# The first batch of an attention-then-network kernel: odd heads on the upper partitions, five first transfers, and a planner that counts transfers in flight

## The chip, the cores and the metric

The kernel runs on one core of one Trainium2 chip. The metric is the device time of one execution in microseconds. Five engines take part, each with its own in-order instruction queue: TensorE (PE; its weight loads are shown apart, as PEld), VectorE (DVE), ScalarE (ACT), GpSimd (POOL) and SyncE (SP), which here issues nearly all transfers from HBM.

## The reference, cut to what matters

Windowed attention with a linear bias for 8 batches of 8 heads, 576 positions and head size 64, then a two-layer network over all 4608 rows:

```python
scores = scale * np.matmul(q, k.transpose(0, 1, 3, 2))
bias = slopes[:, None, None] * (-np.abs(rel).astype(np.float32))[None, :, :]
mask = (rel >= 0) & (rel < window)                    # window = 128
scores = np.where(mask, scores + bias[None], -1000000000.0)
attn = softmax(scores)                                # max, exp, sum + 1e-9
x = np.matmul(attn, v) ...reshape(4608, 512)
h = x @ w_in                                          # 512 x 2048
g = h * (1.0 / (1.0 + np.exp(-1.702 * h)))
out = g @ w_out                                       # 2048 x 512
```

## The kernel before, in words

**The network.** Rows of x are taken in 18 chunks of 256 (a `Job` each; the first chunk is done in two jobs, eight of the sixteen slices of the hidden size in each). One step of a job takes one slice f of 128 hidden units: `up` (twelve matmuls into `h_ps`, L881), the gating on ACT and DVE (L889, L890), the split of g into a high and a low fp32r part (`gh`, `gl`), and `down` (six matmuls into `acc`, L905). x and the weights are split into high and low parts in the same way, so that three fp32r products stand for one fp32 product.

**The weights** arrive as 64-bit words (512 KB a slice and matrix, 32 in all) and are turned into fp32 by `decode`: two steps on ACT (L511, L513), two on DVE (L515, L518), a cast for the high part, and a subtraction for the low part, which may run on POOL or on DVE (L522, by `less_ways`). Decoding of the first two starts when `DECODE_TICK` units of attention have been written down.

**Attention.** Batches 1 to 7 work on pairs of heads in fp32r. Batch 0 is done in plain fp32, head by head, so that the network can begin early: for rows 0 to 255, then 256 to 511, then 512 to 575, eight units of one head each. A unit is: scores (`s_ps` or, for odd heads of the first rows, `s_h`, L694); bias and row minimum on DVE (L712); exponent and row sum on ACT (L724); reciprocal of the sum (L733, L735); scaling (L746 on POOL or DVE, L744 on ACT); transposes on PE (`t_ps`, L767); a copy to SBUF (`turned` or `pw`, L435); times V (`x_ps` or `x_acc`, L806); a copy into x (L850). Here Q and K of batch 0 lie on partitions 0 to 63 for every head. `load_part` fetches them in pieces of two heads (128 KB) and V in pieces of 128 rows (256 KB); the first part takes ten transfers, four of Q and two of V on SP and four of K on ACT, and the second ten on SP. Casts and copies that the planner may move are recorded at L435, such subtractions at L438, halvings at L444. The tiles lie where late weights will come to lie (`home`).

**What sets the order.** `Plan` records every operation with a cost in ns, and `order` (L280) runs through a list schedule of the five engines with these costs up to 130,000 ns of its own time (`CUT`); the instructions are then written out in that order. Its constants decide: `READY` (when an engine is first free), `LAX` (how much longer an operation may take on its first engine than on another before it is moved there), `RATE` (bytes per ns of the transfers), `AHEAD` (how far transfers may be issued ahead), `WARM` (before that time, PE's costs count double), `SLACK` (how many network steps before its due time the attention of a batch should be finished), `FETCH_AHEAD` (how many slices of weights are fetched ahead of decoding). Behind the cut, `rest` hands out the remaining operations and a scheduler places them. Where the plan leaves PE idle before the first `acc` matmul, `spins` fills in bf16 matmuls of the identity matrix (`spin`, L482, tile `idle`), whose result nothing reads, one for every 107 ns, or 214 ns in the first 7 us. They are called spins below.

Of the kernel before, what the change touches and what calls it, by code (L numbers as in the profile page):

```python
# [21 lines left out]
P = 128  # L22
# [11 lines left out]
BIG = 3.0e38  # L34
FAR = 1.0e37
DEPTH = 3
FETCH_AHEAD = 6
DECODE_AHEAD = 1
F0 = 8
SLACK = 4  # L40
DECODE_TICK = 4
AHEAD = 3000
GATE = 6
READY = {"PE": 1600, "DVE": 4400, "ACT": 2100, "POOL": 2700, "SP": 700}
HOP = {"PE": 220, "ACT": 60, "DVE": 60, "POOL": 60, "SP": 60}
CUT = 130000
WARM = 7000
LAX = {"w": 0, "hi": 800, "lo": 2000, "gl": 150, "cast": 100, "xl": 600, "p": 300}
RATE = 330
SOON = 0  # L50
NEXT = 100
SPIN = 107
MIXED = ("t", "o", "h", "acc1")
ENGINES = ("PE", "ACT", "DVE", "POOL", "SP")
# [168 lines left out]
class Plan:  # L223
# [56 lines left out]
    def order(self, until):  # L280

        free = dict(READY)
        port = 0
        wire = 0
        queue = {e: [] for e in ENGINES}
        def ahead(e, op):
            return sum(o.ns for o in queue[e] if o.n < op.n and len(o.ways) == 1)
# [9 lines left out]
        while True:  # L297
            best = None
            for e in ENGINES:
                pick = None  # L300
                for op in queue[e]:
                    at = max(op.ready, free[e], wire - AHEAD if op.bytes else 0)
                    blocked = False
                    for buf in op.opens:
                        if buf.at is None:
                            times = [0 if s is None else (s.done if s.left == 0 else None) for s in buf.slots]
                            times = [t for t in times if t is not None]
                            if not times:
                                blocked = True
                                break  # L310
                            at = max(at, min(times))
                    if blocked:
                        continue
                    ends = at + op.ways[e][0]
                    if any(max(op.ready, free[o] + ahead(o, op)) + op.ways[o][0] + op.lax < ends for o in op.ways if o != e):
                        continue
                    if pick is None or (at, op.n) < pick[:2]:
                        pick = (at, op.n, op)
                if pick:
                    at = max(pick[0], port) if pick[2].ways[e][1] else pick[0]  # L320
                    if best is None or (at, pick[0]) < best[:2]:
                        best = (at, pick[0], pick[2], e)
            if best is None or best[0] >= until:
                break
            at, _, op, op.eng = best
            op.ns, op.port = op.ways[op.eng]
            if op.eng == "PE" and at < WARM:
                op.ns *= 2
            for e in op.ways:
                queue[e].remove(op)  # L330
            for buf in op.opens:
                free_at = [(0 if s is None else s.done, i) for i, s in enumerate(buf.slots) if s is None or s.left == 0]
# [64 lines left out]
def tile_kernel(ctx: ExitStack, tc: tile.TileContext, q0, k0, v0, qT, kT, v, w_in, w_out, out):  # L397
# [16 lines left out]

    def spins(a, b):
        cold = max(min(b, WARM) - a, 0)
        return int(cold // (2 * SPIN) + (b - max(a, min(b, WARM))) // SPIN)

    def act_cast(n):
        return 104 + 0.8 * n  # L420
# [116 lines left out]
            yield hh, c, o, at, m  # L537
            at += m

    homes = [f"w{i}_{f}" for f in range(NF - 1, NF - 12, -1) for i in (1, 2)]  # L540
    parts, values = {}, {}

    def home(shape, name):
        return buf(const, shape, F32, homes.pop(), name=name)

    def load_part(lo, n, on=("SP", "SP")):
        if n == T:
            Q = [home([P, 4, T], f"q{lo}_{i}") for i in range(2)]
            K = [home([P, 4, T], f"k{lo}_{i}") for i in range(2)]
            parts[lo // T] = Q, K  # L550
            V = home([P, 2, DM], f"v{lo}")
            for j in range(2):
                values[lo // P + j] = (V, j), lambda h, j=j: V.t[:, j, h * D:(h + 1) * D]
            for i in range(4):
                for e, (src, to) in zip(on, ((q0, Q), (k0, K))):
                    st = to[i // 2]
                    hs = slice(i % 2 * 2, i % 2 * 2 + 2)
                    piece(e, st, src[:, 2 * i:2 * i + 2, lo:lo + n], lambda t, hs=hs: t[:D, hs], 131072, i % 2)
                if i == 1:
                    for j in range(2):  # L560
                        piece("SP", V, v0[lo + j * P:lo + j * P + P, :], lambda t, j=j: t[:, j], 262144, j)
        else:
            QK = home([P, 2, H, n], f"qk{lo}")
            parts[lo // T] = [QK], [QK]
            V = home([P, DM], f"v{lo}")
            values[lo // P] = (V, 0), lambda h: V.t[:n, h * D:(h + 1) * D]
            piece("SP", QK, q0[:, :, lo:lo + n], lambda t: t[:D, 0], 131072, 0)
            piece("SP", QK, k0[:, :, lo:lo + n], lambda t: t[:D, 1], 131072, 1)
            piece("SP", V, v0[lo:lo + n, :], lambda t: t[:n], 131072, 0)

    def piece(e, dst, src, view, bytes, name):
        on = nc.sync if e == "SP" else nc.scalar
        add(e, lambda: on.dma_start(view(dst.t), src), 550 if e == "SP" else 110, w=[(dst, name)], bytes=bytes,
            chain="first" + e)

    def columns(kind, h, lo, n):
        i, at = divmod(lo, T)
        to = parts[i][kind]
        if len(to) == 2:
            st = to[h // 4]  # L580
            return (st, h // 2 % 2), lambda: st.t[:D, h % 4, at:at + n]
        return (to[0], kind), lambda: to[0].t[:D, kind, h, at:at + n]

    def load(u):
        if u.whole:
# [497 lines left out]
def lay_out(q, k, v, moe_w_in, moe_w_out):  # L1083
# [7 lines left out]
    def words(w):  # L1091
        return np.ascontiguousarray(w).view(np.int64)

    def rows(a):

        return np.ascontiguousarray(np.asarray(a)[0].transpose(2, 0, 1))
# [4 lines left out]
    return {  # L1101
        "q0": rows(q),
        "k0": rows(k),
        "v0": np.ascontiguousarray(v[0].transpose(1, 0, 2)).reshape(S, DM),
        "qT": transposed(q[1:]),
        "kT": transposed(k[1:]),
# [16 lines left out]
```

## Time and profile before

| | |
|---|---|
| median of 3 runs (lowest, highest) | 1073.58 us (1073.49, 1073.8) |
| the profiled execution | 1070.47 us, its span 1068.5 us |
| mean granted TensorE clock | 0.995 |
| PE busy, share of the span | 1054.0 us, 99% |
| DVE, ACT, POOL busy | 737.1, 611.7, 575.5 us |
| first `h_ps` matmul | 39.19 us |

The span runs from the first to the last instruction. A timeline row gives start, duration, engine, line, operation and tiles, and in brackets the idle time before it with what ended it. The granted clock is a share of full speed. A line number is that of the kernel before; "x4" counts instructions. An fp32 matmul shows as two records.

### The profile page before, as it was taken

What the parts mean: (1) busy time and instruction counts of PE and PEld (TensorE: products, weight loads), DVE (VectorE), ACT (ScalarE), POOL (GpSimd) and SP (SyncE); (2) the same over time, 40 slices, a digit from 0 to 9 for tenths busy, and PEclk for the clock granted to TensorE, in tenths of its full rate; (3) what the DMA queues carried; (4) which work ended last, traced back from release to release, by engine and by line L of the source; (5) the groups of instructions that cost most, each with busy time, mean ns of one, the idle gap of its engine ahead of it and who ended that gap; (6) DMA issues with size and microseconds to landing.
All of it is one profiled execution on the core that took longest, in us unless ns stands there. A gap on an engine that the chain in (4) does not pass through costs nothing.

```text
span 1068.5 us, 21819 instructions
## 1 busy us (share of the span) xinstructions
PE 1054.0 (99%) x7044; PEld 943.7 (88%) x7044; DVE 737.1 (69%) x2339; ACT 611.7 (57%) x1817; POOL 575.5 (54%) x871
## 2 busy tenths in 40 slices
PE   8999999999999999999999999999999999999998
PEld 5768899998999899999999998999899989998987
DVE  5999999889886777634778668785878677313121
ACT  5988976666666565524565556655566555322222
POOL 1324576677676666533566557665666565323232
PEclk8999999999999999999999999999999999999999
DMA  9922423333332232201222212221322120000000
GB/s 236 361 81 94 128 73 83 100 81 97 83 90 64 71 88 56 83 9 39 54 86 61 81 54 87 67 84 45 93 67 73 52 66 30 21 1 21 1 21 20
DMA packets 90272, 80.18 MB, mean 75 GB/s; under 512 B 42992, under 2 KB 80880, under 8 KB 90160
## 3 DMA queue, kind: packets, MB, share of 16 engines
q1 hardware_dynamic: 84400, 68.84, 22.4%
q10 hardware_dynamic: 5760, 9.96, 2.6%
q8 instruction: 55, 0.90, 0.3%
q14 instruction: 57, 0.47, 0.1%
HBM read 69.34 MB, written 9.44 MB: 74 GB/s over the span
## 4 chain that ended last, share of the span: by engine, by line
PE 88%; DVE 6%; ACT 3%; issue 2%; DMA 1%; POOL 0%; ACTq 0%; DVEq 0%; SPq 0%
PE h_ps L881 35%; PE acc L905 35%; PE t_ps L767 5%; PE x_ps L812 5%; PE s_ps L697 5%; PE x_ps L806 1%; PE s_ps L694 1%; DVE pb L712 1%; DVE K L435 1%; DVE pb L746 1%; DVE xh L435 1%; DMA k<-k 0%; DMA rw<-w_in 0%; ACT rw L513 0%; DVE xf L852 0%
## 5 line engine op out<-in xcount | busy, mean ns | idle before, releaser
L881 PE MATMUL h_ps<-xh,w 128*128 128x256 f32 x2304 | 371.2, 284 | 2.1 <-DVE rec L733 0.8
L881 PEld LDWEIGHTS h_ps<-xh,w 128*128 128x128 f32 x2304 | 327.8, 188 | 29.1 <-DVE g L890 1.4
L438 POOL TENSOR_TENSOR gl<-g,gh 128x256 fp32r<-128x256 f32 x275 | 204.6, 744 | 269.6 <-ACT gh L435 207.9
L905 PE MATMUL acc<-w,gh 128*128 128x512 f32 x1152 | 325.7, 398 | 0.8 <-ACT gh L435 0.8
L890 DVE SCALAR_TENSOR_TENSOR g<-g,h_ps 128x256 f32<-128x256 f32 x288 | 119.6, 415 | 188.7 <-ACT g L889 187.0
L889 ACT ACTIVATE g<-h_ps 128x256 f32<-128x256 f32 x288 | 110.0, 382 | 204.8 <-PE h_ps L881 176.4
L905 PEld LDWEIGHTS acc<-w,gh 128*128 128x128 f32 x1152 | 195.7, 188 | 27.1 <-ACT gh L435 1.3
L881 PE MATMUL h_ps<-xl,w 128*128 128x256 f32 x1152 | 196.5, 282 | 0.0
L435 ACT CAST gh<-g 128x256 fp32r<-128x256 f32 x283 | 114.5, 405 | 132.1 <-DVE g L890 121.3
L905 PE MATMUL acc<-w,gl 128*128 128x512 f32 x576 | 188.2, 401 | 0.0
L881 PEld LDWEIGHTS h_ps<-xl,w 128*128 128x128 f32 x1152 | 164.4, 188 | 6.6 <-DVE xl L438 0.2
L438 POOL TENSOR_TENSOR K<-rk,K 128x384 fp32r<-128x384 f32 (+1 forms) x140 | 128.0, 915 | 77.2 <-PE s_ps L697 14.5
L724 ACT ACTIVATE pb<-pb,mins 128x256 f32<-128x256 f32 (+3 forms) x276 | 134.2, 487 | 61.3 <-DVE mins L712 59.2
L746 DVE TENSOR_SCALAR pb<-pb,rec 128x256 f32<-128x256 f32 (+2 forms) x244 | 117.0, 513 | 3.7
L712 DVE CUSTOM_DVE_ANT_0 pb<-s_ps,bias 128x256 f32<-128x256 f32 (+2 forms) x304 | 109.4, 377 | 5.5 <-PE s_ps L694 1.9
L438 POOL TENSOR_TENSOR Q<-rq,Q 64x256 fp32r<-64x256 f32 (+1 forms) x140 | 97.3, 695 | 29.2 <-issue 7.2
L905 PEld LDWEIGHTS acc<-w,gl 128*128 128x128 f32 x576 | 94.7, 189 | 9.5
L767 PE MATMUL t_ps<-ident,pb 128*128 128x128 f32 (+2 forms) x524 | 98.2, 273 | 1.6 <-DVE pb L746 0.7
L786 DVE TENSOR_TENSOR pl<-t_ps,ph 128x512 fp32r<-128x512 f32 (+2 forms) x140 | 84.3, 604 | 8.6 <-ACT ph L435 7.5
L697 PE MATMUL s_ps<-K,Q 128*128 128x256 f32 (+1 forms) x504 | 88.4, 288 | 0.1
L733 DVE TENSOR_SCALAR rec<-sums 128x2 f32<-128x2 f32 (+2 forms) x156 | 46.8, 300 | 52.1 <-ACT pb L724 51.6
L435 DVE CAST K<-rk 128x384 fp32r<-128x384 f32 (+1 forms) x133 | 61.6, 463 | 27.3 <-PE s_ps L697 26.3
(93 smaller groups left out, 1281.7 us busy)
## 6 DMA issues: line engine op xcount, KB each, us to landing
rk<-kT SPq DMA_DIRECT2D x84, 192.0 KB, 2.3
rq<-qT SPq DMA_DIRECT2D x112, 128.0 KB, 2.2
out<-o ACTq DMA_DIRECT2D x36, 256.0 KB, 2.2
rw<-w_in SPq DMA_DIRECT2D x16, 512.0 KB, 6.4
rw<-w_out SPq DMA_DIRECT2D x16, 512.0 KB, 7.3
rk<-kT SPq DMA_DIRECT2D x56, 128.0 KB, 2.0
rv<-v SPq DMA_DIRECT2D x100, 64.0 KB, 1.9
rq<-qT SPq DMA_DIRECT2D x28, 64.0 KB, 1.8
```

The costliest lines, as they stand in the source:

```text
L435: (nc.scalar.copy if e == "ACT" else nc.vector.tensor_copy)(dst, src)
L438: (nc.gpsimd if e == "POOL" else nc.vector).tensor_tensor(dst, a, b, ALU.subtract)
L697: nc.tensor.matmul(to, u.Q.t[:, q], ks.t[:, k], start=(z == 0), stop=(z == 1))
L712: add("DVE", lambda b=b, e=e, head=head, ra=ra, rb=rb, cs=cs: nc.vector.tensor_tensor_reduce(b.p.t[ra:rb, cs:b.end], u.s.t[ra:rb, e, cs:b. ...
L724: nc.scalar.activation(live, live, AF.Exp, bias=u.mins.t[:b.rows, e:e + 1], scale=-1.0, accum_out=u.sums.t[:b.rows, e:e + 1])
L746: (nc.gpsimd if on == "POOL" else nc.vector).tensor_scalar(live, live, rec, None, ALU.mult)
L767: nc.tensor.transpose(u.t.t[:c.n, w:w + b.rows], b.p.t[:b.rows, col:col + c.n], ident[:b.rows, :b.rows])
L786: add("DVE", lambda m=m, a=a, z=z: nc.vector.tensor_tensor(u.pl.t[:m, a:z], u.t.t[:m, a:z], u.ph.t[:m, a:z].bitcast(F32), ALU.subtract), d ...
L881: nc.tensor.matmul(h.t, w.t[:, z, k * P:(k + 1) * P], x[k].t, start=(part == 0 and k == 0), stop=(part == 2 and k == NC - 1))
L889: add("ACT", lambda: nc.scalar.activation(g.t, h.t, AF.Tanh, scale=0.851), act_psum(T), r=[h], w=[g], shift=-NEXT)
L890: add("DVE", lambda: nc.vector.scalar_tensor_tensor(g.t, g.t, 1.0, h.t, ALU.add, ALU.mult), dve_one(T), r=[h], w=[g], shift=-NEXT)
L905: nc.tensor.matmul(acc.t, g.t[:, t * P:(t + 1) * P], w.t[:, z], start=(f == self.f0 and n == 0), stop=(f == self.f1 - 1 and n == 2))
```

## The change

Q and K of batch 0 are laid out by the host so that even heads lie on partitions 0 to 63 and odd heads on 64 to 127, all columns of one part of the rows behind each other. The first part then takes five transfers of its own: Q and K in two pieces each (two heads, then six), and V in one. The second part takes three instead of ten, the third three as before. `columns` picks the half by `h % 2`, so that the score matmuls of odd heads read the upper 64 partitions. The planner's model of transfers changes: a transfer costs 100 ns more, and may not start before the eighth transfer back has landed, plus 400 ns. Six constants change, and `spins` gives one spin more for a gap of more than half a spin behind 7 us.

```diff
-FETCH_AHEAD = 6
+FETCH_AHEAD = 5
-SLACK = 4
-DECODE_TICK = 4
+SLACK = 2
+DECODE_TICK = 7
-READY = {"PE": 1600, "DVE": 4400, "ACT": 2100, "POOL": 2700, "SP": 700}
+READY = {"PE": 1600, "DVE": 4400, "ACT": 700, "POOL": 2700, "SP": 700}
-LAX = {"w": 0, "hi": 800, "lo": 2000, "gl": 150, "cast": 100, "xl": 600, "p": 300}
+LAX = {"w": 1500, "hi": 800, "lo": 2000, "gl": 150, "cast": 300, "xl": 300, "p": 300}
-NEXT = 100
+NEXT = 0
...
-        wire = 0
+        wire, landed = 0, []
...
-                    at = max(op.ready, free[e], wire - AHEAD if op.bytes else 0)
+                    at = max(op.ready, free[e])
+                    if op.bytes:
+                        at = max(at, wire - AHEAD, landed[-8] + 400 if len(landed) > 7 else 0)
...
-                wire = max(wire, at + 500) + op.bytes / RATE
+                wire = max(wire, at + 500) + 100 + op.bytes / RATE
                 end = wire + 1500
+                landed.append(end)
...
-        return int(cold // (2 * SPIN) + (b - max(a, min(b, WARM))) // SPIN)
+        n = int(cold // (2 * SPIN) + (b - max(a, min(b, WARM))) // SPIN)
+        return n + (b - a > SPIN // 2 and b > WARM)
...
-            Q = [home([P, 4, T], f"q{lo}_{i}") for i in range(2)]
-            K = [home([P, 4, T], f"k{lo}_{i}") for i in range(2)]
+            Q, K = home([P, NP, T], f"q{lo}"), home([P, NP, T], f"k{lo}")
...
-            for i in range(4):
-                for e, (src, to) in zip(on, ((q0, Q), (k0, K))):
-                    st = to[i // 2]
-                    hs = slice(i % 2 * 2, i % 2 * 2 + 2)
-                    piece(e, st, src[:, 2 * i:2 * i + 2, lo:lo + n], lambda t, hs=hs: t[:D, hs], 131072, i % 2)
+            for a, z in ((0, 1), (1, NP)) if lo == 0 else ((0, NP),):
+                for e, src, to in (("SP", q0, Q), (on, k0, K)):
+                    piece(e, to, src[:, off + a * n:off + z * n], lambda t, a=a, z=z: t[:, a:z], P * (z - a) * n * 4, a > 0)
+            piece("SP", V, v0[lo:lo + n, :].rearrange("(c p) d -> p c d", p=P), lambda t: t, P * 2 * DM * 4, 0)
...
+        rows = slice(h % 2 * D, h % 2 * D + D)
+        key = kind if to[0] is to[1] else h > 1 if i == 0 else 0
+        return (to[kind], key), lambda: view(to[kind].t, kind)[rows, h // 2, at:at + n]
...
-    load_part(0, T, ("SP", "ACT"))
+    load_part(0, T, "ACT")
...
+    def halves(a):
+        a = a[0].reshape(NP, 2, S, D).transpose(1, 3, 0, 2).reshape(P, NP, S)
+        return np.concatenate([a[:, :, lo:min(lo + T, S)].reshape(P, -1) for lo in range(0, S, T)], axis=1)
```

The change moves instructions on every engine. Three places follow; the numbers in a tile's name tell its buffer (`q0` is Q of rows 0 to 255, `rw1_0` and `rw2_0` the raw first slices of w_in and w_out, `work0` to `work3` the scores of two heads each).

SP's queue from its first transfer, before:

```order
L573 DMA q0_0_0_107<-q0 64x2x256 x2
L573 DMA v0_0_110<-v0 128x512 x2
L573 DMA q0_1_0_119<-q0 64x2x256 x2
L413 DMA rw1_0_0_122<-w_in 128x512
L413 DMA rw2_0_0_124<-w_out 128x512
L573 DMA q256_0_0_145<-q0 64x2x256
L573 DMA k256_0_0_154<-k0 64x2x256
L573 DMA q256_0_0_145<-q0 64x2x256
```

and now:

```order
L573 DMA q0_0_109<-q0 128x256
L573 DMA q0_0_109<-q0 128x768
L573 DMA v0_0_113<-v0 128x2x512
L416 DMA rw1_0_0_115<-w_in 128x512
L416 DMA rw2_0_0_130<-w_out 128x512
L573 DMA q256_0_145<-q0 128x1024
L573 DMA k256_0_162<-k0 128x1024
L573 DMA v256_0_190<-v0 128x2x512
```

The first weights move from the seventh and eighth place to the fourth and fifth, and the second part comes in three transfers.

ACT's queue from the exponents of the third head (`work1`), before:

```order
L724 ACTIVATE work1_0_173,numbers_0_151<-work1_0_173,numbers_0_151 128x128
L511 ACTIVATE w_ps_0_191<-rw1_0_0_122 128x512
L744 ACTIVATE work0_0_150<-work0_0_150,numbers_0_151 128x256
L724 ACTIVATE work1_0_173,numbers_0_151<-work1_0_173,numbers_0_151 128x256
L513 ACTIVATE rw1_0_0_122<-rw1_0_0_122 128x512
```

and now, from the exponents of the fifth head (`work2`), the copies of transposed scores among them:

```order
L723 ACTIVATE work2_0_184,numbers_0_136<-work2_0_184,numbers_0_136 128x128
L439 COPY turned0_0_176<-t_ps_1_188 128x384
L723 ACTIVATE work2_0_184,numbers_0_136<-work2_0_184,numbers_0_136 128x256
L723 ACTIVATE work2_0_184,numbers_0_136<-work2_0_184,numbers_0_136 128x128
L439 COPY turned1_0_222<-t_ps_0_202 128x384
L723 ACTIVATE work2_0_184,numbers_0_136<-work2_0_184,numbers_0_136 128x256
L515 ACTIVATE w_ps_0_234<-rw1_0_0_115 128x512
```

The first decode step (L511, now L515) stood between the two exponents of the third head, ahead of the scaling of the second; now it comes behind those of the sixth.

PE's queue from the fourth head's scores, before (LDWEIGHTS and MATMUL of `ident` into `idle` are one spin):

```order
L694 MATMUL s_h_0_167<-k0_0_0_112,q0_0_0_107 128x128
L694 MATMUL s_h_0_167<-k0_0_0_112,q0_0_0_107 128x256
L482 LDWEIGHTS ident_73
L482 MATMUL idle_82<-ident_73 128x256
...
L767 MATMUL t_ps_1_184<-ident_73,work0_0_150 128x128
L482 LDWEIGHTS ident_73
L482 MATMUL idle_82<-ident_73 128x256
L767 MATMUL t_ps_1_184<-ident_73,work0_0_150 128x128 x2
L694 MATMUL s_ps_0_195<-k0_1_0_115,q0_1_0_119 128x128
```

and now:

```order
L693 MATMUL s_h_1_154<-k0_0_107,q0_0_109 128x128
L693 MATMUL s_h_1_154<-k0_0_107,q0_0_109 128x256
L766 MATMUL t_ps_1_164<-ident_73,work0_0_135 128x128 x3
L693 MATMUL s_ps_0_170<-k0_0_107,q0_0_109 128x128
L693 MATMUL s_ps_0_170<-k0_0_107,q0_0_109 128x256
L693 MATMUL s_h_0_179<-k0_0_107,q0_0_109 128x128
L693 MATMUL s_h_0_179<-k0_0_107,q0_0_109 128x256
L766 MATMUL t_ps_1_188<-ident_73,work0_0_135 128x128 x3
```

Between the scores and the transposes of the first heads no spins are left. Over the whole program there are 56 spins before and 66 now: at the very start 16 and now 10, from there to the first `h_ps` matmul 40 and now 51 (in the new order the first two stand behind the values of the third head, the next eight behind the fifth's), and 5 behind it.

More of the change, by code (lines that the diff above doesn't have):

```diff
@@ L538, in spread @@
             at += m
-    homes = [f"w{i}_{f}" for f in range(NF - 1, NF - 12, -1) for i in (1, 2)]
+    homes = [f"w{i}_{f}" for f in range(NF - 1, NF - 10, -1) for i in (1, 2)]
     parts, values = {}, {}
@@ L544, in home, with load_part @@
         return buf(const, shape, F32, homes.pop(), name=name)
-    def load_part(lo, n, on=("SP", "SP")):
+    def load_part(lo, n, on="SP"):
+        off = NP * lo
         if n == T:
-            Q = [home([P, 4, T], f"q{lo}_{i}") for i in range(2)]
-            K = [home([P, 4, T], f"k{lo}_{i}") for i in range(2)]
-            parts[lo // T] = Q, K
+            Q, K = home([P, NP, T], f"q{lo}"), home([P, NP, T], f"k{lo}")
+            parts[lo // T] = (Q, K), lambda t, kind: t
             V = home([P, 2, DM], f"v{lo}")
@@ L552, in load_part @@
             for j in range(2):
-                values[lo // P + j] = (V, j), lambda h, j=j: V.t[:, j, h * D:(h + 1) * D]
-            for i in range(4):
-                for e, (src, to) in zip(on, ((q0, Q), (k0, K))):
-                    st = to[i // 2]
-                    hs = slice(i % 2 * 2, i % 2 * 2 + 2)
-                    piece(e, st, src[:, 2 * i:2 * i + 2, lo:lo + n], lambda t, hs=hs: t[:D, hs], 131072, i % 2)
-                if i == 1:
-                    for j in range(2):
-                        piece("SP", V, v0[lo + j * P:lo + j * P + P, :], lambda t, j=j: t[:, j], 262144, j)
-        else:
-            QK = home([P, 2, H, n], f"qk{lo}")
-            parts[lo // T] = [QK], [QK]
+                values[lo // P + j] = V, lambda h, j=j: V.t[:, j, h * D:(h + 1) * D]
@@ new lines, in load_part @@
+            for a, z in ((0, 1), (1, NP)) if lo == 0 else ((0, NP),):
+                for e, src, to in (("SP", q0, Q), (on, k0, K)):
+                    piece(e, to, src[:, off + a * n:off + z * n], lambda t, a=a, z=z: t[:, a:z], P * (z - a) * n * 4, a > 0)
+            piece("SP", V, v0[lo:lo + n, :].rearrange("(c p) d -> p c d", p=P), lambda t: t, P * 2 * DM * 4, 0)
+        else:
+            QK = home([P, 2, NP, n], f"qk{lo}")
+            parts[lo // T] = (QK, QK), lambda t, kind: t[:, kind]
@@ L565, in load_part @@
             V = home([P, DM], f"v{lo}")
[L566 to L569, printed above, removed]
+            values[lo // P] = V, lambda h: V.t[:n, h * D:(h + 1) * D]
+            piece("SP", QK, q0[:, off:off + NP * n], lambda t: t[:, 0], P * NP * n * 4, 0)
@@ L571, in piece @@
+            piece("SP", QK, k0[:, off:off + NP * n], lambda t: t[:, 1], P * NP * n * 4, 1)
+            piece("SP", V, v0[lo:lo + n, :], lambda t: t[:n], n * DM * 4, 0)
     def piece(e, dst, src, view, bytes, name):
         on = nc.sync if e == "SP" else nc.scalar
-        add(e, lambda: on.dma_start(view(dst.t), src), 550 if e == "SP" else 110, w=[(dst, name)], bytes=bytes,
+        add(e, lambda: on.dma_start(view(dst.t), src), 600 if e == "SP" else 700, w=[(dst, name)], bytes=bytes,
             chain="first" + e)
@@ L577, in columns @@
         i, at = divmod(lo, T)
[L578 to L582, printed above, removed]
+        to, view = parts[i]
+        rows = slice(h % 2 * D, h % 2 * D + D)
+        key = kind if to[0] is to[1] else h > 1 if i == 0 else 0
+        return (to[kind], key), lambda: view(to[kind].t, kind)[rows, h // 2, at:at + n]
     def load(u):
@@ L1092, in words @@
         return np.ascontiguousarray(w).view(np.int64)
-    def rows(a):
-        return np.ascontiguousarray(np.asarray(a)[0].transpose(2, 0, 1))
+    def halves(a):
+        a = a[0].reshape(NP, 2, S, D).transpose(1, 3, 0, 2).reshape(P, NP, S)
+        return np.concatenate([a[:, :, lo:min(lo + T, S)].reshape(P, -1) for lo in range(0, S, T)], axis=1)
     q, k, v = np.asarray(q), np.asarray(k), np.asarray(v)
@@ L1101, in lay_out @@
     return {
-        "q0": rows(q),
-        "k0": rows(k),
+        "q0": np.ascontiguousarray(halves(q)),
+        "k0": np.ascontiguousarray(halves(k)),
         "v0": np.ascontiguousarray(v[0].transpose(1, 0, 2)).reshape(S, DM),
```

## The prediction

> **What bounds the kernel now.** I read first how the span splits over time, because the share of TensorE (99%) is an average over an opening and a long dense part. The view of engine busy time by stretch (columns: us, then busy us and instructions of PE, PEld, DVE, ACT, POOL, then granted clock, DMA share, GB/s):
>
> ```profile
> 10.00:15.00 5.00, 3.76 (x15) 2.29 (x15) 2.70 (x13) 3.06 (x9) 1.16 (x2) 0.80 1.07 275
> 15.00:20.00 5.00, 5.00 (x15) 3.10 (x15) 2.39 (x11) 3.22 (x10) 0.60 (x1) 0.50 1.11 239
> ...
> 40.00:50.00 10.00, 9.58 (x58) 7.72 (x58) 9.76 (x26) 9.48 (x24) 2.71 (x3) 1.00 1.03 410
> 50.00:60.00 10.00, 9.92 (x61) 7.14 (x60) 9.33 (x28) 9.55 (x25) 2.43 (x3) 1.00 0.14 57
> 60.00:80.00 20.00, 19.03 (x118) 13.74 (x117) 18.93 (x57) 17.18 (x45) 5.00 (x5) 1.00 0.30 107
> 80.00:100.00 20.00, 19.22 (x123) 15.63 (x123) 19.23 (x52) 16.75 (x46) 9.96 (x12) 1.00 0.18 48
> 100.00:130.00 30.00, 29.13 (x196) 25.12 (x196) 27.88 (x84) 26.67 (x76) 13.70 (x21) 1.00 0.47 153
> 130.00:900.00 770.00, 766.11 (x5254) 701.55 (x5254) 582.53 (x1895) 457.85 (x1408) 482.82 (x741) 1.00 0.25 70
> ```
>
> From 130 to 900 us PE is idle 770 - 766.11 = 3.9 us: there is little to win. From 40 to 130 it is idle 0.42 + 0.08 + 0.97 + 0.78 + 0.87 = 3.1 us, while VectorE is busy 85.1 of 90. The opening is different: PE is busy by its records, but at half clock. The same view with narrow stretches, PE alone:
>
> ```profile
> 13.00:13.20 0.20, 0.16 (x1) 0.62 1.09 184
> 13.20:23.20 10.00, 10.00 (x31) 0.50 1.11 258
> 23.20:23.30 0.10, 0.10 (x2) 0.55 1.26 151
> ```
>
> So the clock falls at 13.05 and returns at 23.29 us, 10.24 us later, which costs about 5.1 us. What led to it stands in the timeline (start, duration, engine and line):
>
> ```profile
> 11.94 0.62 ACT L511 ACTIVATE w_ps<-rw 128x512 f32<-128x512 f32 x1 [2.58 <-DMA rw<-w_in]
> 12.50 0.49 ACT L744 ACTIVATE work<-work,numbers 128x256 f32<-128x256 f32 x1
> 13.04 0.47 PE L767 MATMUL t_ps<-ident,work 128*128 128x128 f32 x1 [0.94 <-ACT work L744]
> ```
>
> ScalarE stood 2.58 us at the first decode step (L511), waiting for w_in; behind it in its queue was the scaling L744 of the second head, and PE's transpose waited for that. That weight came late because SP issued it late:
>
> ```profile
> 4.20 1.26 SPq L573 DMA_DIRECT2D q<-q  x2
> 6.82 0.33 SPq L413 DMA_DIRECT2D rw<-w_in  x1
> ```
>
> Eight transfers (4 of K, 2 of Q, 2 of V) stand ahead of the one at 4.20. The first K piece, issued at 0.74, lands 3.4 later, at 4.14:
>
> ```profile
> L573 ACTq DMA_DIRECT2D k<-k x1: 724/724/724, 0.7 to 0.7; - x1
> DMA to landing us min/median/max: 3.4/3.4/3.4
> ```
>
> The ninth transfer starts 0.06 us after that: it reads as a limit of eight in flight.
>
> **The change, part by part.** I count to the first matmul of the network's first layer (h_ps). Full-clock prices and that mark, from the timeline of PE and the chain of waits:
>
> ```profile
> 4.89 1.55 PE L694 MATMUL s_ps<-k,q 64*128 64x128 f32 x4
> 7.18 0.92 PE L694 MATMUL s_ps<-k,q 64*128 64x128 f32 x4
> 7.94 0.81 PE L694 MATMUL s_h<-k,q 64*128 64x128 f32 x4
> ```
>
> ```profile
> 15.20 1.58 PE s_ps L694 x4
> 16.78 0.83 PE t_ps L767 x3
> 17.61 1.47 PE x_acc L806 x4
> ...
> 24.60 1.07 PE s_ps L694 x6
> 25.67 0.79 PE x_acc L806 x4
> 26.47 0.32 PE idle L482 x2
> 26.79 0.33 PE t_ps L767 x3
> ...
> 31.35 1.53 PE idle L482 x14
> 34.22 0.44 PE t_ps L767 x4
> ...
> 39.19 2.54 PE h_ps L881 x20
> 41.73 1.01 PE x_ps L806 x6
> ```
>
> A head of the first 256 rows costs 7.94 - 7.18 = 0.76 (scores) + 0.33 (transposes) + 0.79 (values) = 1.88 us, eight heads 15.0. Before, PE had also done four score blocks of the second part (4.3), two sets of transposes (0.9) and one of values (1.0) by 39.19: 21.2 us of work, so 18.0 us were lost.
>
> In the new order PE does the 15.0, three score blocks (3.2) and one set of transposes (0.44) ahead of h_ps: 18.7. Its losses:
> - **Start.** The first score needs the first piece of Q and of K, 128 KB each as before, so I keep 4.14 and take 4.2 (before 4.89, when the sixteen spins ended).
> - **Warm-up.** If the clock rises at about 6.2, as the score times of before say (1.55 us at 4.89, 0.82 to 0.92 from 6.28), two microseconds at half clock cost 1.0.
> - **Spins.** Behind the start stand 51 spins ahead of h_ps (before 40). At 1.53 / 14 = 0.109 each: 5.6.
> - **Stall and slow clock.** ScalarE's first decode step comes behind the exponents of six heads; SP has issued w_in as its fourth transfer, not its seventh. Issued no later than 4.20 + 0.6, and landing after 5.1 as before (issued at 6.82, used at 11.94), it is there by 10, and this wait goes to nothing. Next in line are the scalings, which POOL and VectorE share; VectorE was busy 2.70 of 5 in that stretch. I put 0.5 for gaps. If this cover fails, another 0.9 us (the wait above) and 5.1 are back.
>
> Sum: 18.7 + 4.2 + 1.0 + 5.6 + 0.5 = 30.0, so 11.3 lost instead of 18.0: **-6.7 us**.
>
> Between h_ps and 130 us, seventeen of the low halves of the weights move from VectorE to POOL (25 and 7 before, 8 and 24 now):
>
> ```profile
> L438 DVE TENSOR_TENSOR w<-wc,w 128x512 fp32r<-128x512 f32 x25 | 18.3, 731 | 0.2
> L438 POOL TENSOR_TENSOR w<-wc,w 128x512 fp32r<-128x512 f32 x7 | 9.2, 1316 | 18.5 <-ACT w L435 7.5 <-ACT w_ps L511 6.4 <-DVE rec L735 3.0
> ```
>
> That takes 17 x 0.731 = 12.4 us off the engine that is full there, and adds 22.4 to one that is busy 34 of 90. At best it removes PE's 3.1 us of idle; at worst every half arrives 1.316 - 0.731 = 0.6 us later on the path, +9.9. I take -1.5, near the idle row, because decoding runs ahead of use. Five more spins there: +0.5. Pacing with less slack (SLACK 2), fewer weights ahead and the new order far behind: bounded by the 3.9 us of idle either way, taken as 0. The odd heads' matmuls on the upper rows have the same shapes; nothing in this trace shows such operands. The score work is 8 x 0.76 = 6.1, so between -1 (overlap where a low head meets a high one) and +1; taken as 0.
>
> Total: -6.7 - 1.5 + 0.5 = **-7.7**. The profiled execution took 1070.47 (span 1068.5 and 2.0 around it); 1062.8 on that scale. The runs without the profile have their median 3.1 us higher, at 1073.58; I carry the difference over: **1065.9**.
>
> [...] The row first: the two switches lie 10.24 us apart, three times 3.41, and PE is busy by its records from 13.04 on, yet two such stretches passed without a return. The returning stretch differs by half a microsecond of bf16 spins, begun here:
>
> ```profile
> 22.75 1.85 PE L482 MATMUL idle<-ident 128*128 128x256 bf16 x13
> ```
>
> [...]
>
> **The rivals.**
> 1. *The clock stays low, and it gets slower (0.22).* Ten spins at 3.59 / 16 = 0.224 end at 3.6; PE pauses to 4.2, and then runs only fp32 work, which did not raise the clock from 13 to 22:
>
> ```profile
> 0.00:5.00 5.00, 3.59 (x16) 1.00 0.45 114
> ```
>
> At half clock seven more scores, four sets of transposes and three of values follow the first score: 8 x 1.58 + 4 x 0.83 + 3 x 1.47 = 20.4, so 24.6, and two spins in the next stretch raise it, about 26.7. From there remain half a value set (0.3), 49 spins (5.3), three score blocks (3.2), the other values and transposes (4 x 0.79 + 3 x 0.33 + 0.44 = 4.6): h_ps at about 40.1, 21.4 lost, +3.4. With the -1.0 of later: +2.4, 1076.0. It decides at the first 3.4 us step behind the spins. Against: counted back from 13.05, steps fall at 6.2 and 2.8; half a microsecond of spins was enough in the stretch before 23.29, and between 2.8 and 6.2 lie 0.8.
> 2. *The clock rises late, near 16.5 (0.15).* Three steps at half clock cost 3 x 1.7 = 5.1: -2.6, 1071.0.
> 3. *ScalarE gives it back (0.10).* From 40 to 130 us it is busy 79.6 of 90. If its queue sets that stage, only its own 2.58 us come back: 1071.0.
>
> **How the numbers follow.** The forecast has 0.48; 0.05 is left for what I did not name. About 0.2% (2.1 us) is what a measurement of this kernel can tell from no change. Below 1071.4 lie the forecast (0.48), about two thirds of the second and half of the third rival: 0.63. Within: 0.17. Slower: 0.20. The range goes from the forecast with all the idle of 40 to 130 gone and 1.8 of the 3.9 us behind it (1062.5) to the first rival (1076.0). The forecast's own range is 1062.5 to 1069.
>
> **What would show it.** Right: ScalarE's first decode step without a wait; the clock at 1.00 from 10 to 25 us; h_ps near 30; VectorE's busy share down by about 12 us from 30 to 130. Wrong: score blocks of 1.5 us behind 6.2, a granted clock of 0.5 from 6 to 27, h_ps at 38 or later; or h_ps early and PE idle over 6 us from 40 to 130 with waits for decoded weights.

## The result, and the profile after

| | before | after |
|---|---|---|
| median (lowest, highest), us | 1073.69 (1073.49, 1075.08) | 1060.03 (1059.04, 1060.49) |
| runs | 4 | 4 |
| profiled execution, its span, us | 1070.47, 1068.5 | 1059.04, 1057.3 |
| first `h_ps`, us | 39.19 | 31.62 |
| PE, DVE, POOL busy, us | 1054.0, 737.1, 575.5 | 1046.5, 717.9, 590.2 |

The ratio is 0.9869, with a 95% interval from 0.9852 to 0.9886. The kernel became 13.7 us faster; the forecast was 7.7, and 1060.03 lies below its range. Lines of the changed kernel are one or two lower than before (L693 are the scores, L880 is `h_ps`), the decode steps four higher (L515).

The view of busy time by stretch, of the changed kernel (us, then busy us and instructions of PE, PEld, DVE, ACT, POOL, then granted clock, DMA share, GB/s):

```profile
10.00:15.00 5.00, 5.00 (x23) 2.99 (x22) 3.20 (x18) 3.39 (x13) 1.47 (x2) 0.82 1.04 407
15.00:20.00 5.00, 5.00 (x29) 3.00 (x29) 4.45 (x19) 4.58 (x14) 1.50 (x2) 1.00 1.09 308
40.00:50.00 10.00, 9.84 (x59) 7.65 (x58) 9.34 (x28) 9.89 (x25) 4.21 (x4) 1.00 0.56 221
50.00:60.00 10.00, 9.19 (x54) 6.38 (x53) 8.40 (x23) 8.81 (x23) 3.31 (x3) 1.00 0.00 0
60.00:80.00 20.00, 20.00 (x126) 15.27 (x126) 18.17 (x56) 18.24 (x50) 11.99 (x12) 1.00 0.24 75
80.00:100.00 20.00, 20.00 (x130) 16.48 (x130) 18.03 (x47) 17.00 (x46) 9.47 (x10) 1.00 0.22 71
100.00:130.00 30.00, 29.95 (x207) 26.40 (x206) 28.63 (x89) 28.27 (x83) 18.31 (x23) 1.00 0.41 129
130.00:900.00 770.00, 766.98 (x5282) 705.24 (x5281) 565.42 (x1890) 455.34 (x1404) 480.40 (x738) 1.00 0.25 70
```

From 40 to 130 us PE's idle time is 1.0 us, where it was 3.1, and POOL is busy 47 us, where it was 34. VectorE has lost 2.6 us of busy time there, not twelve: its low halves fell from 13.8 to 5.3 us, but the scalings rose from 3.2 to 5.0, and the rest of the room went to small changes in other groups. Behind 130 us the idle time has hardly changed (3.0 for 3.9), though the stretch holds 28 matmuls more.

The clock still falls and returns, but for 3.41 us. PE alone, in narrow stretches around the two switches:

```profile
8.40:8.50 0.10, 0.10 (x3) 0.54 0.70 287
8.41:11.82 3.41, 3.41 (x15) 0.50 1.02 411
11.80:11.90 0.10, 0.10 (x1) 0.90 0.98 369
```

The row reads 0.50 for these 3.41 us, where before it did for 10.24. ScalarE's first decode step has no wait in brackets any more, and SP issues w_in at 2.13:

```profile
14.69 0.62 ACT L515 ACTIVATE w_ps<-rw 128x512 f32<-128x512 f32 x1
```

```profile
1.66 0.43 SPq L573 DMA_DIRECT2D v<-v  x1
2.13 0.47 SPq L416 DMA_DIRECT2D rw<-w_in  x1
```

PE's timeline shows what the forecast had taken as nothing. `s_ps` is the first head (lower rows), `s_h` the second (upper rows):

```profile
3.81 0.58 PE L693 MATMUL s_ps<-k,q 64*128 64x128 f32 x1
3.83 0.58 PE L693 MATMUL s_h<-k,q 64*128 64x128 f32 x1
...
4.40 0.63 PE L693 MATMUL s_ps<-k,q 64*128 64x256 f32 x1
4.41 0.63 PE L693 MATMUL s_h<-k,q 64*128 64x256 f32 x1
...
6.25 0.89 PE L693 MATMUL s_ps<-k,q 64*128 64x128 f32 x4 [0.96 <-DVE numbers L711]
7.23 0.92 PE L693 MATMUL s_h<-k,q 64*128 64x128 f32 x4
...
8.65 0.58 PE L693 MATMUL s_ps<-k,q 64*128 64x128 f32 x1
8.66 0.58 PE L693 MATMUL s_h<-k,q 64*128 64x128 f32 x1
...
9.66 0.63 PE L693 MATMUL s_ps<-k,q 64*128 64x256 f32 x1
9.68 0.63 PE L693 MATMUL s_h<-k,q 64*128 64x256 f32 x1
```

The two heads' matmuls start 0.01 to 0.02 us apart and run side by side. The pair at 8.65 lies wholly at half clock and ends at 10.31: two heads take 1.66 us, as long as one head alone takes at half clock (1.65, in the run with the pairs split below). The heads at 6.25 and 7.23 do not overlap (the first ends at 7.14); the fourth head's scores go into the same buffer as the second's, and wait for VectorE to finish with it.

The network starts, and the first and the last pair of results leave, at these times in the changed kernel:

```profile
31.62 1.19 PE L880 MATMUL h_ps<-xh,w 128*128 128x256 f32 x8
...
146.25 0.36 ACTq L928 DMA_DIRECT2D out<-o  x1
...
1053.56 0.94 ACTq L928 DMA_DIRECT2D out<-o  x2
```

and in the kernel before:

```profile
157.40 0.35 ACTq L929 DMA_DIRECT2D out<-o  x1
...
1064.57 0.94 ACTq L929 DMA_DIRECT2D out<-o  x2
```

So 7.6 us are won by the first `h_ps`, 11.2 by the first result and 11.0 by the last. Up to the first `h_ps` PE has 18.7 us of work as the prediction counted it, so 31.6 - 18.7 = 12.9 are lost instead of 18.0: the opening gives 5.1 at equal work. The other 5.9 of the profiles' 11.0 come behind it, where the prediction had 1.0.

### The profile page after: what moved, and what is told of

Same layout as the page of the kernel before. It is cut to its first block, busy times and chain, and to the rows that moved or that the text cites. A ratio compares the mean times of both kernels' runs of the same rounds, so it can differ in the third digit from the quotient of the medians.

```text
span 1057.3 us, 21848 instructions
## 1 busy us (share of the span) xinstructions
PE 1046.5 (99%) x7054; PEld 941.5 (89%) x7054; DVE 717.9 (68%) x2327; ACT 612.5 (58%) x1823; POOL 590.2 (56%) x877
## 4 chain that ended last, share of the span: by engine, by line
PE 93%; DMA 3%; DVE 2%; issue 1%; POOL 1%; ACT 1%; SPq 0%; DVEq 0%; POOLq 0%
PE h_ps L880 37%; PE acc L904 37%; PE x_ps L811 5%; PE s_ps L696 5%; PE t_ps L766 5%; DMA rw<-w_in 1%; PE x_ps L805 1%; DMA v<-v 1%; PE s_ps L693 1%; DMA rw<-w_out 1%; POOL w L442 0%; DVE pb L745 0%; SPq L416 0%; DVE rec L732 0%; DVE pb L711 0%
## 5 line engine op out<-in xcount | busy, mean ns | idle before, releaser
L880 PE MATMUL h_ps<-xh,w 128*128 128x256 f32 x2304 | 368.1, 284 | 1.3 <-DVE g L889 1.1
L880 PEld LDWEIGHTS h_ps<-xh,w 128*128 128x128 f32 x2304 | 327.0, 188 | 29.0 <-DVE g L889 2.1
L439 ACT CAST gh<-g 128x256 fp32r<-128x256 f32 x288 | 116.7, 405 | 145.8 <-DVE g L889 135.6
L880 PE MATMUL h_ps<-xl,w 128*128 128x256 f32 x1152 | 194.3, 280 | 0.0
L880 PEld LDWEIGHTS h_ps<-xl,w 128*128 128x128 f32 x1152 | 163.9, 188 | 6.3
L745 DVE TENSOR_SCALAR pb<-pb,rec 128x256 f32<-128x256 f32 (+2 forms) x251 | 109.2, 469 | 3.5
L766 PE MATMUL t_ps<-ident,pb 128*128 128x128 f32 (+2 forms) x524 | 94.6, 272 | 0.7 <-DVE pb L745 0.7
L696 PEld LDWEIGHTS s_ps<-K,Q 128*128 128x128 f32 x504 | 74.1, 189 | 6.1 <-DVE mins L711 0.6
```

What stands on the lines that cost most here:

```text
L439: (nc.scalar.copy if e == "ACT" else nc.vector.tensor_copy)(dst, src)
L696: nc.tensor.matmul(to, u.Q.t[:, q], ks.t[:, k], start=(z == 0), stop=(z == 1))
L745: (nc.gpsimd if on == "POOL" else nc.vector).tensor_scalar(live, live, rec, None, ALU.mult)
L766: nc.tensor.transpose(u.t.t[:c.n, w:w + b.rows], b.p.t[:b.rows, col:col + c.n], ident[:b.rows, :b.rows])
L880: nc.tensor.matmul(h.t, w.t[:, z, k * P:(k + 1) * P], x[k].t, start=(part == 0 and k == 0), stop=(part == 2 and k == NC - 1))
```

## The experiments

Theory 1, from the two traces: the opening gave 5.1, the low halves taken off VectorE 3.3, the pace (SLACK) 2.7, all of it behind 150 us. Its rivals: layout and transfers bring nearly all of it, or the planner's numbers do.

**Numbers and layout apart.** The changed kernel with the old numbers, and the kernel before with the new ones:

```diff
-FETCH_AHEAD = 5
+FETCH_AHEAD = 6
-SLACK = 2
-DECODE_TICK = 7
+SLACK = 4
+DECODE_TICK = 4
-READY = {"PE": 1600, "DVE": 4400, "ACT": 700, "POOL": 2700, "SP": 700}
+READY = {"PE": 1600, "DVE": 4400, "ACT": 2100, "POOL": 2700, "SP": 700}
-LAX = {"w": 1500, "hi": 800, "lo": 2000, "gl": 150, "cast": 300, "xl": 300, "p": 300}
+LAX = {"w": 0, "hi": 800, "lo": 2000, "gl": 150, "cast": 100, "xl": 600, "p": 300}
-NEXT = 0
+NEXT = 100
```

The second run has the same lines the other way round, with the new model of transfers and the new spin rule.

> The changed kernel with all the planner's numbers of before (FETCH_AHEAD 6, SLACK 4, DECODE_TICK 4, READY ACT 2100, LAX w 0, cast 100, xl 600, NEXT 100); layout, five transfers, the counting of transfers in flight and the spin rule stay. Theory 1, from the two traces: the opening gives 5.1 us, the stage to about 150 us 3.3 (the low halves off VectorE), the rest of the span 2.7 (the pace). Then about 1060.0 + 3.3 + 2.7 = 1066, with the first h_ps near 32 to 36 and VectorE's busy time back up by about 19 us. Rival (layout): the transfers and the layout bring nearly all, then 1060 to 1062. Rival (numbers): the planner's numbers bring nearly all, then 1070 to 1074.

> The kernel before with the new numbers, the counting of transfers in flight and the new spin rule; old layout and ten transfers. Theory 1: 1073.7 - 3.3 - 2.7 = about 1067.7, with the first h_ps still near 39. Rival (layout): 1072 to 1075. Rival (numbers): 1060 to 1063, and the first h_ps near 32.

Measured: 1069.28 us (1067.6 to 1070.95) with the old numbers, ratio to before 0.9965 [0.995, 0.9981], first `h_ps` at 34.05; 1073.14 (1072.38 to 1074.61) with the new numbers on the old layout, ratio 1.0004 [0.9989, 1.0018], first `h_ps` at 42.42. No theory had both: alone they bring 4.4 and 0.5 us, together 13.7. (With the old numbers the planner puts 25 spins at the very start, and the first score comes at 6.70.) The timeline of PE in the second run says why the new numbers brought nothing there. Ten spins end at 3.7, and then scores and values run at half speed until the spins at 28 to 31 us:

```profile
4.63 1.62 PE L698 MATMUL s_ps<-k,q 64*128 64x128 f32 x4 [0.95 <-DMA q<-q]
...
29.52 1.54 PE L810 MATMUL x_ps<-turned,v 128*64 128x256 f32 x4
30.99 0.96 PE L486 MATMUL idle<-ident 128*128 128x256 bf16 x6
31.89 0.86 PE L810 MATMUL x_acc<-turned,v 128*64 128x256 f32 x4
```

The four records of a set of values take 1.54 at 29.52 and 0.86 at 31.89. This is the course of the prediction's first rival, on the old layout. The granted clock of this run reads 1.00 from 4 to 31 us all the same, with a head's scores at 1.62 us: here the view showed a fall (0.50 behind 8.41 in the changed kernel), and not a clock that had not yet risen.

**One number at a time.** LAX w at 0 (low halves go where they are done first), and SLACK at 4:

```diff
-LAX = {"w": 1500, "hi": 800, "lo": 2000, "gl": 150, "cast": 300, "xl": 300, "p": 300}
+LAX = {"w": 0, "hi": 800, "lo": 2000, "gl": 150, "cast": 300, "xl": 300, "p": 300}
```

```diff
-SLACK = 2
+SLACK = 4
```

> The changed kernel with LAX w at 0, so that low halves of weights go where they are done first, as before. Theory 1: most of the 3.3 us of the stage to 150 us is lost again: about 1063, VectorE up by 10 us or more, TensorE's idle time from 40 to 130 us up from 1.0 to about 3. Rival (the low halves are hidden anyway, the gain of that stage comes from the pace and the earlier weights): within 0.7 us of 1060.

> The changed kernel with SLACK 4 as before. Theory 1: the 2.7 us behind 150 us are the pace's, so about 1062.7, all of it lost behind 150 us. Rival (the late gain has another source, such as where POOL's low halves stand, or is the order's chance): within 0.7 us of 1060.

Measured: 1066.73 us (1064.37 to 1071.09) and 1064.14 (1063.64 to 1065.13). For SLACK the size is near what theory 1 said, 4.1 for 2.7 (4.6 to 5.4 between runs of one granted clock). PE alone from 480 to 900 us, in the changed kernel, with SLACK 4, and before:

```profile
480.00:900.00 420.00, 419.59 (x2885) 1.00 0.23 65
```

```profile
480.00:900.00 420.00, 418.56 (x2864) 1.00 0.23 65
```

```profile
480.00:900.00 420.00, 418.49 (x2866) 1.00 0.23 66
```

With SLACK 2 PE gets some 20 records further in the same time, about 2.9 us of work at this rate, and only 1.0 us of that is idle time in the records; the rest is a slightly closer sequence. All kept traces agree, whatever else differs: 2879 to 2887 records in the twelve with SLACK 2, 2864 to 2868 in the six with SLACK 4. But the place is not theory 1's alone: by 150 us PE has 936 records in the changed kernel and 909 with SLACK 4, so part of the loss has arisen before, 1.1 us of it by the first `h_ps` (32.71), where this execution's clock rose late. For LAX w the loss of 6.7 is twice what was expected, and PE's idle time from 40 to 130 did not rise (0.9 us), so it is not what theory 1 said.

**The pairs.** Theory 2, the author's guess from the runs above: the clock returns only in a 3.41 us step (the distance of the switches after; before, 10.24 is three of them) whose matmuls fill enough of the array's rows, and it is the overlapping heads that fill them. One spin put between the two heads of each pair keeps these two apart; the order of all else stays. (The second and the third head then overlap for 1.2 us, from 6.0 on, at half clock.)

```diff
...
-                    spin(spins(at, op.start))
+                    spin(spins(at, op.start) + (1 if firsts in (1, 3, 8) else 0))
+                    firsts += 1
```

> The changed kernel with one spin (128x256 bf16, all rows) put between the scores of a low head and those of the high head behind it, for the three such pairs of heads 0 to 5, so that no two score blocks lie side by side; nothing else moves. Theory 2, from the first four runs: the clock comes back only in a 3.41 us step whose matmuls fill enough of the rows, and it is the pairs that fill them; without them half clock holds to the first stretch of spins, near 20 to 31 us as in the run with new numbers and the old layout, the first h_ps comes 3 to 6 us later and the time is 1063 to 1066. Rival: the pairs save only their own overlap, 3 x 1.4 us at half clock, most of it under VectorE; the clock returns at about 13.4 as in the runs without the split, and the time is 1060 to 1061.5.

Measured: 1067.02 us (1066.89 to 1068.76), 7.0 more than the changed kernel and 1.0 above theory 2's range; the first `h_ps` at 39.83, 8.2 later where 3 to 6 were expected, and later than in the kernel before (39.19). About 1.0 of these are the three added spins themselves (0.3 to 0.4 each at half clock). PE's timeline in this run:

```profile
16.57 1.65 PE L693 MATMUL s_ps<-k,q 64*128 64x128 f32 x4
18.15 0.69 PE L766 MATMUL t_ps<-ident,work 128*128 128x128 f32 x2
18.77 1.54 PE L805 MATMUL x_acc<-turned,v 128*64 128x256 f32 x4
20.24 1.65 PE L693 MATMUL s_h<-k,q 64*128 64x128 f32 x4
...
24.12 0.61 PE L486 MATMUL idle<-ident 128*128 128x256 bf16 x2
24.52 0.85 PE L766 MATMUL t_ps<-ident,work 128*128 128x128 f32 x3
25.30 1.04 PE L805 MATMUL x_acc<-turned,v 128*64 128x256 f32 x4
```

and its busy time in one stretch:

```profile
5.00:25.00 20.00, 20.00 (x61) 1.00 1.03 380
```

PE is busy in all of these 20 us and still runs at half speed (a head's scores 1.65), until the values at 25.30. Without the overlap the clock is some 12 us later than in the run with SLACK 4 and the run without spins below, where the pairs overlap and it rises near 13.5. So 20 us at work by the records did not bring the clock back here; the rival, which gave the pairs only their own overlap, is out. Nor did it take bf16 spins: in the run without spins none stands between 3.7 us and the rise near 13.5. That it is the filled rows that count was not shown: no run changed them alone. An estimate from the timelines of the kept traces, which counts time with one half of the rows at work as half, fits nearly all runs: the 3.41 us steps in which PE was at work throughout and the clock stayed low come to 0.61 to 0.85 (before, those from 13.05 and 16.46 to 0.81 and 0.85), those at whose end it rose to 0.87 or more (before, the one up to 23.29 to 0.90; after, those up to 5.0 and 11.82 to 0.96 and 1.00), but for one of 0.82 (the first rise of the kernel before).

**The spins, and the clock.** The ten opening spins alone; and, in another run, the fourth head's scores in the free buffer, with four spins in PE's pause ahead of the third head:

```diff
-                    spin(spins(at, op.start))
+                    spin(spins(at, op.start) if op.start < 5000 else 0)
```

```diff
...
-                buf.at = max(fits)[1]
+                buf.at = (min if buf.tag == "h" and at < 9000 else max)(fits)[1]
...
-                    spin(spins(at, op.start))
+                    spin(spins(at, op.start) + (4 if firsts == 2 else 0))
+                    firsts += 1
```

> The changed kernel with its ten opening spins alone; the 51 behind them up to the first h_ps and the 5 behind that are left out, the order of all else is the same. The prediction priced the spins at 0.109 each on the path, 5.6 us: by that, 1054 to 1055. Theory 2: the spins stand where TensorE waits anyway (for VectorE, ScalarE and the first weights), so at most 1 us comes back; the clock may fall in a step with too little work, which costs up to 2: 1059 to 1062, with the first h_ps between 31 and 34.

> The changed kernel with the fourth head's scores in the other buffer of h, so that heads 2 and 3 can run side by side too, and four spins ahead of the third head's scores, where TensorE stood 0.7 to 1.0 us. Theory 2: the rows are filled from 1.4 us on, the clock rises between 4.8 and 8.2 whatever the phase of the step, instead of near 13.4; half of that stretch, 2.5 to 4 us of TensorE's time, comes back as far as VectorE and ScalarE keep up: 1057 to 1059.5. Rival (the opening is VectorE's and ScalarE's, not TensorE's): 1060, the first h_ps within 0.5 us.

Measured: 1056.12 us (1055.95 to 1057.4) without the later spins, first `h_ps` at 30.51; 1057.63 (1057.26 to 1060.01) with the second buffer, first `h_ps` at 30.15. The first is neither the prediction's 5.6 nor theory 2's 1: between runs of one granted clock it is 2.4 to 3.1 us. Part of the spins stand where PE waits; in the run without them:

```profile
21.68 0.52 PE L766 MATMUL t_ps<-ident,work 128*128 128x128 f32 x3 [0.47 <-DVE numbers L734]
22.86 0.52 PE L766 MATMUL t_ps<-ident,work 128*128 128x128 f32 x3 [0.66 <-ACT turned L439]
```

The clock stayed up in these pauses of 0.47 and 0.66 us: three transposes take 0.52 behind them, and took 0.90 at half clock (those of the changed kernel that start at 10.24 us). The second is as theory 2 had it: the third and the fourth head now overlap and run at full clock from 6.17 on.

```profile
5.20 1.04 PE L486 MATMUL idle<-ident 128*128 128x256 bf16 x4
6.17 0.38 PE L693 MATMUL s_ps<-k,q 64*128 64x128 f32 x1
6.18 0.37 PE L693 MATMUL s_h<-k,q 64*128 64x128 f32 x1
```

Both together, with ten and four spins (the line for the buffer is as above):

```diff
...
-                    spin(spins(at, op.start))
+                    spin(10 if firsts == 0 else 4 if firsts == 2 else 0)
+                    firsts += 1
```

> The two best edits together: the fourth head's scores in the other buffer of h, ten opening spins and four ahead of the third head's scores, and none of the other spins. If the clock's early return (2.4 us) and the spins left out (3.9) are separate: 1060.0 - 2.4 - 3.9 = 1053.7, the first h_ps at 27 to 28.5. Rival (behind both stands the same chain of VectorE, ScalarE and the first weights): 1055.5 to 1056.5, the first h_ps near 30. Rival (with gaps in TensorE's work the clock falls again): 1058 or more, and a granted clock below 0.997.

Measured: 1054.69 us (1054.54 to 1057.1), ratio to before 0.983 [0.9805, 0.9856]: faster than both kernels, 1.0 short of the full sum.

```profile
27.67 1.18 PE L880 MATMUL h_ps<-xh,w 128*128 128x256 f32 x8
```

**The old layout with more spins.** The kernel before with the new numbers (lines as above), and 24 opening spins instead of ten:

```diff
...
-                    spin(spins(at, op.start))
+                    spin(spins(at, op.start) if firsts else 24)
+                    firsts += 1
```

> The kernel before with the new numbers, transfer counting and spin rule (old layout), and 24 opening spins in place of 10. With ten its clock rose only at about 31 us. Theory 2: 24 spins, 1.4 to 6.6 us, fill a whole step whatever its phase; the first scores come 2 us later and the following 23 us of matmuls run at full clock: 1061 to 1066, the first h_ps at 33 to 36. Rival (the slow opening is not what held that kernel): 1072 to 1075.

Measured: 1073.02 us, in two groups: ten runs from 1072.69 to 1073.9 with a granted clock of 0.990 to 0.992, and two of 1062.97 and 1063.1 at 0.999 and 1.000. In the profiled one, of the larger group, the clock is up at 5.74 and down again from 11.6 to 28.7, five steps of 3.41:

```profile
5.74 0.92 PE L698 MATMUL s_ps<-k,q 64*128 64x128 f32 x4
...
16.40 1.65 PE L698 MATMUL s_ps<-k,q 64*128 64x128 f32 x4
```

So the median is the rival's, and theory 2 was wrong that 24 spins secure the clock: it is up behind them (0.92 at 5.74), and falls at 11.6 under the heads that follow. Its time (1061 to 1066) came only in the two runs where, by their reading, the clock held. On the old layout it held, by the readings, in these two of the twelve runs and not in the other ten, and that is worth 10 us (1063.0 for 1073.0); where it held, the old layout with the new numbers comes within 3 us of the changed kernel.

**The low halves with the order kept.** In the changed kernel's own order, the first seventeen that the planner gave POOL run on VectorE:

```diff
...
+            if op.eng == "POOL" and op.lax == LAX["w"] and moved < 17:
+                op.eng, moved = "DVE", moved + 1
```

> The changed kernel, its order word for word, but the first seventeen low halves of weights that the planner gave POOL run on VectorE, as many as before the change; each stands in VectorE's queue where the planner's order has it. Theory 1 (VectorE's relief is the gain of the stage to 150 us): 1063 to 1066, TensorE idle 3 us or more from 40 to 130. Rival (what the run with LAX w at 0 lost, 6.7 us, came from the other order that the planner then finds): 1060 to 1061.5.

Measured: 1061.05 us (1059.8 to 1061.68), 1.0 more than with the halves on POOL, though the runs of the two overlap. PE's idle time from 40 to 130 us is 1.5, not 3. Theory 1 falls here; what LAX w at 0 lost beyond that is another order, not VectorE's load.

**The old numbers without spins, and the first decode step.**

```diff
...
-                    spin(spins(at, op.start))
+                    spin(0 if firsts else 10)
+                    firsts += 1
```

```diff
-DECODE_TICK = 7
+DECODE_TICK = 4
```

> The changed kernel with the planner's numbers of before, as in the run with old numbers (1069.3), and ten opening spins alone in place of 101. If spins cost what they did in the changed kernel (3.9 us for 56): about 4 to 6 less, 1063.5 to 1065.5, and that is what layout and transfers are worth without the numbers: 8 to 10 us. Rival (the old numbers' spins fill waits that are there anyway): 1068 to 1070.

> The changed kernel with DECODE_TICK 4 as before, so that the first decode step stands ahead of the later heads' exponents again. If the earlier w_in alone took the 2.58 us wait away: 1060 within 1 us, ScalarE's first decode step without a wait. If it was the place behind the heads: ScalarE waits 1 to 2 us for w_in, the first h_ps comes 2 us later or more, 1062 to 1064.

Measured: 1068.73 us (1065.84 to 1074.65), 0.5 less than with 101 spins, as the rival had it: there they do fill waits, and without them the clock falls again. In the profiled run PE stands 1.26 us ahead of 31.31, and at 33.99 six records of values take 1.91 us, which take 1.08 at 44.14; the granted clock of the twelve runs is 0.986 to 0.999, with 101 spins 0.996 to 1.000. Layout and transfers without the numbers are worth 4.4 to 5.1 us. DECODE_TICK 4: 1068.96 us (1067.51 to 1074.16), outside both expectations. ScalarE's first decode step has no wait there either:

```profile
9.28 0.63 ACT L515 ACTIVATE w_ps<-rw 128x512 f32<-128x512 f32 x1
```

so the earlier w_in alone took the 2.58 us away. The first `h_ps` comes 2.1 later, and from 34 to 130 us PE waits 2.6 us for decoded weights. The remaining 4 us lie further on, where the order is another; they were not taken apart.

**The chance of an order.** The planner lays out 130 us; what follows is taken in program order. Only this cut is moved, on both kernels:

```diff
-CUT = 130000
+CUT = 120000
```

(140000 in the other two runs.)

> The changed kernel with CUT 120000 in place of 130000: the planner lays out 10 us less, the rest follows in program order. Nothing that the change is about is touched, only the order of what comes behind 110 us. Theory 3 (some of the gain is the chance of one order: the changed kernel happens to pass the change of chunk at 300 to 320 us almost without a wait, 0.8 us, where three kernels with other orders stood 2.2 to 2.6 and lost 3 to 5): 1062 to 1066, the first h_ps as before within 0.3 us. Rival (the gain belongs to the numbers and the layout, whatever the order): within 1 us of 1060.

> The changed kernel with CUT 140000: as with CUT 120000, on the other side. Theory 3: 1062 to 1066, TensorE idle 2 us or more from 300 to 320. Rival: within 1 us of 1060.

> The kernel before with CUT 120000. Theory 3: it moves by 1 to 5 us to either side of 1073.7; rival: within 1 us.

> The kernel before with CUT 140000. Theory 3: it moves by 1 to 5 us to either side of 1073.7; rival: within 1 us.

Measured, medians:

| CUT | before | after | difference |
|---|---|---|---|
| 120000 | 1075.98 (1075.08 to 1078.06) | 1065.23 (1063.52 to 1065.99) | -10.8 |
| 130000 | 1073.69 | 1060.03 | -13.7 |
| 140000 | 1070.95 (1065.02 to 1073.65) | 1061.61 (1059.94 to 1062.22) | -9.3 |

A number that has nothing to do with the change moves either kernel by 1.6 to 5.2 us, as theory 3 had it in three of the four runs (the changed kernel with CUT 140000 lies 0.4 below its range). The medians of the kernel before also carry its mix of granted clocks. One place where orders differ is the change of chunk at 300 to 320 us; with CUT 120000, and then in the changed kernel:

```profile
300.00:320.00 20.00, 17.40 (x109) 15.36 (x108) 19.46 (x61) 12.80 (x42) 13.85 (x22) 0.91 0.38 109
```

```profile
300.00:320.00 20.00, 19.55 (x139) 1.00 0.34 96
```

PE is idle 2.6 us in the one and 0.45 in the other, and in the first the granted clock dips as well, to 0.91 in the mean of the 20 us. That is about what 3.41 us at half clock give, and by this estimate it costs 1.7. With CUT 140000 PE is idle 2.5 there too, and the run loses only 1.6 in all, so that place is not the whole of it. The change itself is worth 9 to 14 us, 11.2 in the mean of three orders.

## Why the prediction was right or wrong

The direction was right, and the size 6 us short. Two terms that were taken as 0 failed: the overlap of heads on opposite halves, and the pace. By its own steps:

- **Start (4.2).** Measured 3.81. The first K piece lands 3.0 after its issue, not 3.4.
- **Stall (goes to nothing).** Right: no wait at the first decode step, because w_in is issued at 2.13. The run with DECODE_TICK 4 shows that the earlier transfer does it, not the place behind the heads.
- **Slow clock (rises at 6.2 and stays).** Wrong in its reason. Ten spins did not secure the clock: on the old layout it rose only at 31 us, as the first rival said, and on the new one with the pairs split at 25. In the profiled run of the changed kernel it rose near 5.0, fell at 8.41 and returned at 11.82, so the sign that the prediction named (1.00 from 10 to 25 us) failed. Behind the first score 4.6 us ran at half clock, a loss of 2.3 where the warm-up had 1.0.
- **Upper-row matmuls (taken as 0, bounds -1 to +1).** Wrong: the split measured the term at -7.0 us, some -6 without its own spins, the largest of all. The bound counted the time that overlap saves and not the clock, which returned at 11.82 with the pairs side by side and at 25.3 with them split. The overlap made good what the step above had assumed for another reason, so it is luck that the sum of the opening came out near the truth, -5.1 for -6.7. In the trace the matmuls of the two heads of a pair start 0.01 to 0.02 us apart.
- **Spins (5.6 and 0.5).** Too dear: leaving them out gives 2.4 to 3.9 us, since some stand in waits.
- **Low halves (-1.5).** Right in kind and nearly in size: 1.0 with the order kept, though the two kernels' runs overlap.
- **Pacing and the new order far behind (taken as 0, within 3.9 of idle either way).** This is the step that failed for the size, together with the next. SLACK alone is worth 4.1, and one order against another up to 5.2. PE's idle time did not bound it, because of the 2.9 us gained from 480 to 900 only 1.0 shows as idle time; the rest lies between records that the view counts as busy.
- **The difference between profile and median, 3.1, carried over.** Wrong by 2.1: the changed kernel's median is 1.0 above its profiled execution. The 3.1 seems to have belonged to the clock in that one execution: its reading was 0.995, and the three runs beside the experiments with this reading took 1070.0 to 1070.7. In the 87 runs of the kernel before that ran beside the experiments, three took 1065.6 to 1066.7 us with a granted clock of 0.999 or 1.000, and the rest 1070 to 1077 (some of these at a reading of 1.000 as well, which fits a clock that rose late, as in the run with the new numbers); the changed kernel had its four runs within 1.5 us. That its opening depends less on where the 3.41 us steps happen to begin is the author's guess at the reason, and was not tested.

Taken together: -5.1 (opening), -1.0 (low halves) and -4.1 (SLACK) make 10.2, near the 11.2 of the mean over three orders. The three come from different runs and scales, so this is a rough sum. Read the other way, the kernel with the pairs split is still 6.7 faster than before, and their overlap brings the other 7.0. About 2.5 of the measured 13.7 go with this one order; which instructions make them up was not settled.

## What to carry to other kernels

A row that says PE is busy, and a granted clock of 1.00, did not say here that the array ran at full speed (20.00 of 20 us busy, and a head's scores at 1.65 us for 0.92): look at what one matmul of a known shape takes, from the first one on. Here the clock stayed down for some 20 us (5 to 25, pairs split) under a mix whose scores use 64 of the 128 partitions. With two such heads side by side on opposite halves, two took 1.66 us at half clock, as long as one, and the clock was back at 11.82. Where a planner writes the order, move a number that should not matter before a difference of less than 5 us is put down to the change.

## What the runs showed of the hardware

- In the changed kernel the fp32 score matmuls of two heads, one on partitions 0 to 63 and one on 64 to 127, overlapped: at half clock two heads took 1.66 us (8.65 to 10.31), where one took 1.65 in the run with the pairs split. The second head's first one started (3.83) ahead of the first head's second one (4.40), which stands before it in the program.
- In the run with the pairs split, with score matmuls on half of the rows among its work, PE was busy 20.00 of 20 us (5 to 25) at half speed (a head's scores 1.65 us, 0.92 at full clock), and the view read 1.00.
- The clock's switches lay 10.24 us apart before (13.05 and 23.29), 3.41 after (8.41 and 11.82) and 17.1 on the old layout with 24 spins (11.6 and 28.7), about three, one and five times 3.41. They did not stand at the same times in the two profiled runs: from 8.41 to 13.05 there are 4.64 us, no multiple of 3.41.
- The transfers moved 407 GB/s from 10 to 15 us in the changed kernel, with Q and K on 128 partitions in pieces of 384 and 512 KB, and 275 in the kernel before, with Q and K on 64 partitions in pieces of 128 KB. Which of the two does it was not tried.
